# Attention with both couples' weighing in one run, and another set of rebuilt weights in layer one

## The chip, the cores and the metric

One core of a Trainium2 chip runs the whole program. The metric is the device time in microseconds (us) of one execution; the kernel before was run three times, and its median is 843.62 us. A profile was taken of one further execution.

## The reference

Attention with a sigmoid instead of a softmax is followed by two dense layers. All arrays are float32, except the weights, which are float64 because they were scaled by a float64 number.

```
scores = scale * (q @ k^T) - log(448)          # 4 batches x 12 heads, 448 tokens, 64 wide
x = sigmoid(scores) @ v                        # -> 1792 tokens x 768
h = max(x @ w1, x @ w2, x @ w3);  x = h @ w_out               # 768 -> 768 -> 768
h = x @ w_in;  x = (h * sigmoid(1.702 * h)) @ w_out           # 768 -> 2048 -> 768
```

## The kernel before

**Products.** A float32 operand is cut into a high half (a copy in the type fp32r) and a low half (the rest, by a subtraction). Three fast products, high x high, high x low and low x high, stand for one product. The dense layers use a scheme of seven products instead of eight for a 2 x 2 block product, on sums of weight blocks. Attention weighs the values with sigmoids in full float32 (a slower form of product, in several passes).

**The attention** works on couples. A couple is two heads of one batch; 24 couples form 12 periods of two, X (even number) and Y (odd). I count periods from 0. A period has these runs on TensorE:
- `score(c)` for c = 0, 1, 2 (L590 in the profile of before): scores of 3 x 128 keys, two heads side by side, from the high and low halves of q and k; three products for each c, each for two heads. Their result lies in two of six PSUM banks, taken in turn, and `sigmoid` (L625, ScalarE) reads it from there.
- `score_last` (L642): the 64 last keys of X and of Y together, from the raw float32 tiles.
- `weigh_last` (L653): the values of the last keys of the pair of couples before, added to their sums.
- `weigh(c)` for c = 0, 1, 2 (L609): the sigmoids of the 3 x 128 keys times the values v, summed in one PSUM bank for X and one for Y. `give` copies that bank to SBUF when all parts are in.

Beside that, ScalarE or VectorE make the halves of q and k of the next couples (a copy L309 and a subtraction L312, 848 columns), and both engines turn 18 float64 weight tiles into float32 (`single`: L357 on ScalarE, then L367, L364, L368 and L372 on VectorE). Such a tile arrives by a load of 768 KB (L353), and is stored as yk (L294). The raw q and k tiles and the v tiles have three buffers each, used in turn.

**The layers** follow: layer one and layer two for half of the tokens, then both for the other half, then the wide layers in four quarters. In layer one there are nine sets of seven operands from weight blocks. The first half makes them and stores them (`kept`, 384 KB each); the second half loads them again. The sets in `REDO` are not stored; the second half makes them again from yk (one load of 768 KB).

**What sets the order.** The kernel first records all operations, with what each reads and writes. Those of TensorE are chained in the order in which the code records them. A planner (`Order.run`) then goes through an estimate of time: on each engine the operation that is ready and has the smallest latest start (`late`) is issued next. `late` is taken backwards from the operations that need it, or is the given `at` (for conversions: the planned time of TensorE where they were recorded, plus 5.5). A load's `lag` is how long after its end the planner holds it to be usable. Each engine then executes its list in order; DMAs are issued by SyncE (SP), in its order.

Of the kernel before, what the change touches and what calls it, by code (L numbers as in the profile page):

```python
# [17 lines left out]
B, H, S, D = 4, 12, 448, 64  # L18
# [23 lines left out]
LAND, LAND_RAW = 1.0, 2.0  # L42
MM, FULL = 0.201, 0.752
# [148 lines left out]
BUS = 350.0  # L192
# [8 lines left out]
LEAD = 2  # L201
READY = 1
AHEAD = 5.5
REDO = (1, 3, 5, 7)
AGAIN = (1, 3, 5, 7)
CONV1, CONV2 = 4, 10
WITHIN = 1.4
# [2 lines left out]
def moe_chain_kernel(tc, qk, vv, wa, wb, out):  # L210
    nc = tc.nc
    act, dve, pe, sp = nc.scalar, nc.vector, nc.tensor, nc.sync
    scale = 1.0 / math.sqrt(D)
    O = Order()
# [31 lines left out]
    def F(at, n):  # L246
        if at >= FAR2:
            return Reg(sn4, at - FAR2, n, lambda: slab_n[2][:, at - FAR2 : at - FAR2 + n])
        if at >= FAR:
            return Reg(sn1, at - FAR, n, lambda: slab_n[0][:, at - FAR : at - FAR + n])  # L250
        return Reg(sf, at, n, lambda: slab_f[:, at : at + n])
# [4 lines left out]
    def R(at, n):  # L256
        if at >= FAR2:
            return Reg(sn3, at - FAR2, n, lambda: slab_n[1][:, at - FAR2 : at - FAR2 + n])
        if at >= RW:
            return Reg(s2, at - RW, n, lambda: slab_m[1][:, at - RW : at - RW + n])  # L260
        return Reg(sr, at, n, lambda: slab_r[:, at : at + n])
# [4 lines left out]
    def banks(first, n=1, w=S):  # L266
        cut = (lambda: psum[:, first, :w]) if n == 1 else (lambda: psum[:, first : first + n, :w])
        return Reg(sps, first * 512, n * 512, cut)

    class Round:  # L270


        def __init__(self, places):
            self.places, self.i = list(places), 0
# [21 lines left out]
            [to] if writes is None else writes,  # L296
        )

    def load(to, src, kb, after=(), at=None):
        return O.op({"SP": kb / BUS}, lambda e: sp.dma_start(to(), src), (), [to], after, at)  # L300

    def on(e, took, fn, reads, writes):
        return O.op({e: took}, lambda _: fn(), reads, writes)
# [1 line left out]
    def copy(to, of, n, psum=False, both=True):  # L305
        engines = {"ACT": t_act(n)}
        if both:
            engines["DVE"] = t_two(n) if psum else t_one(n)
        return O.op(engines, lambda e: (act.copy if e == "ACT" else dve.tensor_copy)(to(), of()), [of], [to])  # L309
# [4 lines left out]
    def sub(to, a, b, n):  # L314
        return two(to, a, b, ALU.subtract, n)
# [86 lines left out]
    def moving(base, t=None, at=(None,) * 7):  # L402
        b11, b12, b21, b22 = (base + 3 * i * T for i in range(4))
        t = base + 12 * T if t is None else t
        cuts = ((0, 2), (2, 1))

        def combine(to, x, y):
            for j, n in cuts:
                sub(*(F(z + j * T, n * T) for z in (to, x, y)), n * T)

        m = {k: Moving(x) for k, x in zip(("b11", "t1", "t2", "b21", "t3", "b22", "t4"), at)}
        m["b11"].fill(b11)
        combine(t, b12, b11)
        m["t1"].fill(t)
        combine(b11, b22, t)
        m["t2"].fill(b11)
        m["b21"].fill(b21)
        combine(b12, b22, b12)
        m["t3"].fill(b12)
        m["b22"].fill(b22)  # L420
        combine(b21, b21, b11)
        m["t4"].fill(b21)
        return [m[k] for k in ("b11", "t1", "t2", "b21", "t3", "b22", "t4")]
# [132 lines left out]
    class Couple:  # L556


        def __init__(self, p):
            self.p = p  # L560
            t = t_at()
            h, l = q_at()
            cuts = [(Q, QK, QT), (0, 2 * P, 2 * P), (2 * P, Q, Q)] if p == 0 else [(0, QK, QT)]
            self.parts = []
            for start, stop, end in cuts:
                n = stop - start
                to, tp, hp, lp = F(t + start, end - start), F(t + start, n), R(h + start, n), R(l + start, n)
                self.load = load(to, qk[p][:, start:end], (end - start) / 2, at=-9.0 if p == 0 else None)
                copy(hp, tp, n)
                sub(lp, tp, hp, n)  # L570
                self.parts.append((hp, lp))
            self.t, self.h, self.l = F(t, QT), R(h, QK), R(l, QK)
            self.av = banks(6 + p % 2)
            self.a, self.sc = {}, {}

        def values(self):
            self.v = F(v_at(), 8 * D)
            load(self.v, vv[self.p].rearrange("p c d -> p (c d)"), 256)
# [20 lines left out]
            self.a[c] = sigmoid(self.sc[c])  # L599

        def weigh(self, c):
            ps, v, second = self.av, self.v, self.p % 2 == 1
            begin, end = c == 0 and not second, c == 2 and second

            def f(_):
                w, o, x = v().rearrange("p (c d) -> p c d", d=D), ps(), self.a[c]()
                for e in range(2):
                    r = slice(e * D, (e + 1) * D)
                    pe.matmul(o[r], w[:, 2 * c + e], x[:, e * S : (e + 1) * S], start=begin, stop=end)  # L609

            O.pe(f, FULL + (0 if c else 0.15), [v, self.a[c]] + ([] if begin else [ps]), [ps])
            if end:
                self.give()

        def give(self):
            b, hp = divmod(self.p, NPAIR)
# [3 lines left out]
    def sigmoid(ps):  # L620
        a = M1(a_at(), 2 * S)
        on(
            "ACT",
            t_act(2 * S) + 0.07,
            lambda: act.activation(  # L625
                a().rearrange("p (e s) -> p e s", e=2), ps(), AF.Sigmoid, bias=bias, scale=scale
            ),
            [ps],
            [a],
        )  # L630
        return a

    def score_last(two):

        ps = banks(d_at(), 2)

        def f(_):
            o = ps()
            for c, x in enumerate(two):
                for e in range(2):  # L640
                    r, t = slice(e * D, (e + 1) * D), x.t()
                    pe.matmul(o[c * D : (c + 1) * D, e, :], t[r, QK:QT], t[r, Q:QK], start=True, stop=True)  # L642

        O.pe(f, FULL, [x.t for x in two], [ps])
        return ps

    def weigh_last(two, a):
        def f(_):
            x = a()
            for c, y in enumerate(two):  # L650
                w, o, k = y.v().rearrange("p (c d) -> p c d", d=D), y.av(), slice(c * D, (c + 1) * D)
                for e in range(2):
                    pe.matmul(  # L653
                        o[e * D : (e + 1) * D], w[k, 6 + e], x[k, e * S : (e + 1) * S], start=c == 1, stop=c == 0
                    )

        O.pe(f, FULL + 0.15, [a, two[0].av, *(y.v for y in two)], [y.av for y in two])
        two[0].give()

# [24 lines left out]
    def convert(c):  # L686
        p = c.p - LEAD
        if 0 <= p < 18:
            soon(lambda: prepare(p // 2, p % 2, at=XA + 12 * T if c.p % 3 == 2 else None, after=[c.load]))

    prev, last = None, None
    for i in range(NP // 2):
        x = Couple(2 * i)
        x.values()
        if i == 0:
            x.score(0, slice(0, 1))
            x.score(1, slice(0, 1))
            x.score(0, slice(1, 3))
            x.scored(0)
            x.score(1, slice(1, 3))  # L700
            x.scored(1)
        for n in range(0 if i else 2, 3):
            x.score(n)
            x.scored(n)
        convert(x)
        if prev:
            weigh_last(prev, last)
        y = Couple(2 * i + 1)
        y.values()
        last = sigmoid(score_last((x, y)))  # L710
        for n in range(3 if prev else 0):
            prev[1].weigh(n)
        for n in range(3):
            y.score(n)
            y.scored(n)
        convert(y)
        for n in range(3):
            x.weigh(n)
        prev = (x, y)
    weigh_last(prev, last)  # L720
    for n in range(3):
        prev[1].weigh(n)
    O.rows, O.row = False, []
    gate["m"] = O.op({"-": 0.0}, to_m2, after=set(s1.ops))

# [6 lines left out]
    def layer1(x, first, base, extra=()):  # L732
        sets = []
        for m in range(HK):
            for e in range(3):
# [13 lines left out]
                def weights(i=3 * m + e):  # L749
                    if first or i not in REDO:  # L750
                        return Weights(i, first, sums(), keep=i not in REDO)
                    at = again()
                    return Weights(i, True, at + 2 * DM, y=at, keep=False)
# [21 lines left out]
    x = moving(XA)  # L775
# [3 lines left out]
    x = moving(XB)  # L779
    extra = []  # L780
    for fp in range(EARLY):
        for n in range(2):
            extra.append(lambda fp=fp, n=n: prepare(12 + fp, n, "ACT"))
        if fp < READY:
            w = []
# [298 lines left out]
```

## Time and profile before

| | |
|---|---|
| median of 3 runs | 843.62 us (842.98 to 843.77) |
| the profiled execution's own time | 844.5 us |
| its span, first to last instruction | 842.7 us |
| TensorE busy (PE) | 836.4 us, 4447 matmuls |
| VectorE busy (DVE) | 697.3 us |
| ScalarE busy (ACT) | 538.7 us |
| granted clock of TensorE | 1.00 |

Attention lasts until 132.35 us, layer one's second pass is about 278 to 393 us. Times in the views are from the start of the span. A matmul in full float32 shows as several records; products on different parts of the array run beside each other, so the records of a run overlap, and the start of the next run is what counts.

### The profile page before, as it was taken

The numbers are of one execution on the slowest core, as the hardware profiler recorded it, in microseconds if no ns is written. First come the engines' busy times: TensorE is split into PE (matmuls) and PEld (weight loads), VectorE is DVE, ScalarE is ACT, GpSimd is POOL, SyncE is SP. The second block draws the span as 40 slices with busy tenths as digits, with TensorE's granted clock in tenths as the row PEclk, the third lists the DMA queues.
The fourth block names the chain that finished last, engine by engine and source line by source line (L and its number), as shares of the span: only waits on it lengthen the run. The fifth ranks groups of instructions, "written<-read, shape, count | busy, mean of one in ns | idle before, by whom it ended". The sixth has DMA issues, their size and how long they took to land. (4 is left out here: it accounts for less than half of the span.)

```text
span 842.7 us, 12281 instructions
## 1 busy us (share of the span) xinstructions
PE 836.4 (99%) x4447; PEld 726.2 (86%) x4447; DVE 697.3 (83%) x1009; ACT 538.7 (64%) x756; POOL 0.3 (0%) x5
## 2 busy tenths in 40 slices
PE   8999999999999999999999999999999999999998
PEld 4555557999999999999999999999899999999997
DVE  5898898888899877789788899968977889865785
ACT  7899898566475745666658665776657865344430
POOL 0000000000000000000000000000000000000000
PEclk9999999999999999999999999999999999999999
DMA  8899977877558999789999961993349997863033
GB/s 299 294 365 320 370 276 254 307 253 250 206 187 326 389 351 376 283 296 363 406 386 365 409 247 57 360 373 132 108 155 361 345 423 259 289 238 94 0 99 131
DMA packets 73788, 231.83 MB, mean 275 GB/s; under 512 B 8192, under 2 KB 20864, under 8 KB 71936
## 3 DMA queue, kind: packets, MB, share of 16 engines
q1 hardware_dynamic: 73728, 231.05, 75.0%
q8 instruction: 35, 0.57, 0.3%
q14 instruction: 25, 0.20, 0.1%
HBM read 149.82 MB, written 81.20 MB: 274 GB/s over the span
## 5 line engine op out<-in xcount | busy, mean ns | idle before, releaser
L492 PE MATMUL ps<-r 128*128 128x448 f32 x2250 | 454.6, 362 | 0.0
L492 PEld LDWEIGHTS ps<-r 128*128 128x128 f32 x2250 | 421.7, 187 | 28.9 <-issue 0.7
L312 DVE TENSOR_TENSOR r<-f,r 128x384 fp32r<-128x384 f32 (+4 forms) x235 | 163.0, 711 | 24.3 <-ACT r L309 22.7
L309 ACT CAST r<-f 128x384 fp32r<-128x384 f32 (+4 forms) x199 | 124.2, 649 | 45.3 <-PE ps L492 22.4
L309 ACT COPY f<-ps 128x448 f32<-128x448 f32 x132 | 70.6, 537 | 91.8 <-PE ps L492 73.7
L312 DVE TENSOR_TENSOR f<-f 128x384 f32<-128x384 f32 (+4 forms) x140 | 103.5, 759 | 5.7 <-ACT f L849 4.7
L312 DVE TENSOR_TENSOR f<-ps,f 128x448 f32<-128x448 f32 (+1 forms) x117 | 71.6, 616 | 42.2 <-PE ps L492 31.2
L909 PE MATMUL ps<-n,m 128*128 128x448 f32 x432 | 90.8, 362 | 0.0
L909 PEld LDWEIGHTS ps<-n,m 128*128 128x128 f32 x432 | 81.0, 188 | 5.4
L625 ACT ACTIVATE m<-ps,bias 128x896 f32<-128x896 f32 x84 | 79.1, 1006 | 8.6 <-PE ps L590 7.2
L362 ACT ACTIVATE f<-f 128x768 uint8<-128x768 uint32 x38 | 74.7, 1965 | 0.5
L909 PE MATMUL ps<-r,m 128*128 128x448 f32 x288 | 61.4, 363 | 0.4 <-DVE r L312 0.4
L609 PE MATMUL ps<-m,f 128*64 128x448 f32 x288 | 59.4, 548 | 0.0
L909 PEld LDWEIGHTS ps<-r,m 128*128 128x128 f32 x288 | 53.8, 188 | 4.8 <-DVE r L312 1.1
L492 PE MATMUL ps<-m,r 128*128 128x448 f32 x270 | 57.7, 362 | 0.0
L590 PEld LDWEIGHTS ps<-r 64*128 64x128 f32 x432 | 38.4, 184 | 21.1 <-ACT m L625 9.5
L372 DVE SCALAR_TENSOR_TENSOR f<-f 128x768 uint32<-128x768 uint32 x56 | 53.3, 952 | 2.1 <-ACT f L362 1.8
L492 PEld LDWEIGHTS ps<-m,r 128*128 128x128 f32 x270 | 50.6, 187 | 3.4
L357 ACT ACTIVATE f<-f 128x768 f32<-128x768 f32 x56 | 50.8, 911 | 3.7 <-DMA f<-in_wb 2.9
L590 PE MATMUL ps<-r 64*128 64x448 f32 x432 | 50.7, 374 | 1.1 <-DVE r L309 1.1
L309 ACT COPY ps<-ps 128x448 f32<-128x448 f32 x52 | 27.9, 537 | 35.0 <-PE ps L492 30.2
L312 DVE TENSOR_TENSOR r<-n,r 128x384 fp32r<-128x384 f32 (+3 forms) x65 | 46.5, 724 | 3.2 <-ACT r L309 2.5
(64 smaller groups left out, 640.2 us busy)
## 6 DMA issues: line engine op xcount, KB each, us to landing
r<-kept SPq DMA_DIRECT2D x91, 384.0 KB, 6.0
kept<-r SPq DMA_DIRECT2D x84, 384.0 KB, 5.5
f<-in_wb SPq DMA_DIRECT2D x32, 768.0 KB, 6.9
f<-in_wa SPq DMA_DIRECT2D x24, 768.0 KB, 6.8
yk<-f SPq DMA_DIRECT2D x40, 384.0 KB, 5.1
f<-yk SPq DMA_DIRECT2D x17, 768.0 KB, 6.1
f<-y SPq DMA_DIRECT2D x32, 384.0 KB, 6.9
zs<-r SPq DMA_DIRECT2D x7, 1344.0 KB, 13.1
```

The lines of the kernel that those rows point to most:

```text
L309: return O.op(engines, lambda e: (act.copy if e == "ACT" else dve.tensor_copy)(to(), of()), [of], [to])
L312: return on("DVE", t_two(n), lambda: dve.tensor_tensor(to(), a(), b(), op=op), [a, b], [to])
L357: on("ACT", t_act(DM), lambda: act.activation(y(), words(raw(), F32, 1), AF.Copy, scale=2.0**-112), [raw], [y])
L362: act.activation(byte(), words(raw(), U32, 0), AF.Copy, scale=LOW)
L372: lambda: dve.scalar_tensor_tensor(u(), words(raw(), U32, 1), 0x80000007, u(), **by),
L492: pe.matmul(o, a[:, c], b, start=fresh and j == n == 0, stop=j == HK - 1 and n == 2, skip_group_check=True,)
L590: pe.matmul(o[:, e, :], kx[r, c * P : (c + 1) * P], qx[r, Q:QK], start=n == 0, stop=n == 2)
L609: pe.matmul(o[r], w[:, 2 * c + e], x[:, e * S : (e + 1) * S], start=begin, stop=end)
L625: lambda: act.activation(a().rearrange("p (e s) -> p e s", e=2), ps(), AF.Sigmoid, bias=bias, scale=scale),
L909: pe.matmul(o, a, b, start=fresh and k == n == 0, stop=k == 3 and n == 2, skip_group_check=True)
```

## The change

The order of recording in a period changes: after the scores of Y come the weighings of X and of Y, in one run. Before, the weighing of Y was recorded one period later, behind that period's `score_last`. So a couple's last keys are now added after its other keys (`weigh_last` ends the sum instead of opening it), and both `give` copies follow it. The loads of couple 0 are marked as first of all, and the planner's lag for couple 1's load is larger. `REDO` holds the even sets. The other lines of the kernel are the same.

```diff
-REDO = (1, 3, 5, 7)
+REDO = (0, 2, 4, 6, 8)
...
-                self.load = load(to, qk[p][:, start:end], (end - start) / 2, at=-9.0 if p == 0 else None)
+                self.load = load(to, qk[p][:, start:end], (end - start) / 2, at=-99.0 if p == 0 else None, lag=LAND + 1.2 if p == 1 else None)
...
         def weigh(self, c):
-            ps, v, second = self.av, self.v, self.p % 2 == 1
-            begin, end = c == 0 and not second, c == 2 and second
+            ps, v, begin = self.av, self.v, c == 0
...
-                    pe.matmul(o[r], w[:, 2 * c + e], x[:, e * S : (e + 1) * S], start=begin, stop=end)
-
-            O.pe(f, FULL + (0 if c else 0.15), [v, self.a[c]] + ([] if begin else [ps]), [ps])
-            if end:
-                self.give()
+                    pe.matmul(o[r], w[:, 2 * c + e], x[:, e * S : (e + 1) * S], start=begin, stop=False)
+
+            O.pe(f, FULL + (0 if c or self.p % 2 else 0.15), [v, self.a[c]] + ([] if begin else [ps]), [ps])
...
-                        o[e * D : (e + 1) * D], w[k, 6 + e], x[k, e * S : (e + 1) * S], start=c == 1, stop=c == 0
+                        o[e * D : (e + 1) * D], w[k, 6 + e], x[k, e * S : (e + 1) * S], start=False, stop=True
...
-        O.pe(f, FULL + 0.15, [a, two[0].av, *(y.v for y in two)], [y.av for y in two])
-        two[0].give()
+        O.pe(f, FULL + 0.15, [a, *(z for y in two for z in (y.v, y.av))], [y.av for y in two])
+        for y in two:
+            y.give()
...
-        for n in range(3 if prev else 0):
-            prev[1].weigh(n)
         for n in range(3):
             y.score(n)
             y.scored(n)
         convert(y)
-        for n in range(3):
-            x.weigh(n)
+        for z in (x, y):
+            for n in range(3):
+                z.weigh(n)
         prev = (x, y)
     weigh_last(prev, last)
-    for n in range(3):
-        prev[1].weigh(n)
```

The lines behind it move up by some: L590 stays, L609 becomes L608, L642 L639, L653 L650, L625 L622, L909 L904; L309, L312, L357 to L372 and L492 stay.

TensorE's list over one period in the attention, before (ps are PSUM banks, r the halves, f and n the raw tiles and values, m the sigmoids):

```order
L590 MATMUL ps<-r 128x448 x18
L653 MATMUL ps<-m_76,f 64x448 x4
L642 MATMUL ps<-f 64x448 x4
L609 MATMUL ps<-m_76,f 64x448 x6
L590 MATMUL ps<-r 128x448 x18
L609 MATMUL ps<-m_76,f 64x448 x6
```

The same period in the changed kernel:

```order
L590 MATMUL ps<-r 128x448 x18
L650 MATMUL ps<-m_76,f 64x448 x4
L639 MATMUL ps<-f 64x448 x4
L590 MATMUL ps<-r 128x448 x18
L608 MATMUL ps<-m_76,f 64x448 x12
```

The weighing that stood between the last scores and Y's scores now stands behind X's weighing.

VectorE's list around the halves of couple 21 (Y of period 10), before: the high half was a copy on ScalarE, and the first row of 848 columns is its low half.

```order
L372 SCALAR_TENSOR_TENSOR f<-f 128x768
L312 TENSOR_TENSOR r<-f,r 128x848
L309 COPY n_77<-ps 128x448
L367 TENSOR_SCALAR f<-f 128x768
L364 TENSOR_SCALAR f<-f 128x768
L368 TENSOR_SCALAR f<-f 128x768
```

VectorE's list at the same couple in the changed kernel: CAST is couple 21's high half, the row of 848 columns behind it its low half.

```order
L372 SCALAR_TENSOR_TENSOR f<-f 128x768
L309 CAST r<-f 128x848
L367 TENSOR_SCALAR f<-f 128x768
L364 TENSOR_SCALAR f<-f 128x768
L368 TENSOR_SCALAR f<-f 128x768
L312 TENSOR_TENSOR r<-f,r 128x848
L372 SCALAR_TENSOR_TENSOR f<-f 128x768
```

Three steps of the conversion of another tile now stand between the two halves.

ScalarE's list in period 10 of the changed kernel, from the end of period 9's sigmoids on (three sigmoids, then the conversion copy that ends period 9, then period 10):

```order
L622 ACTIVATE m_76<-ps,bias 128x896 x3
L357 ACTIVATE f<-f 128x768
L622 ACTIVATE m_76<-ps,bias 128x896
L357 ACTIVATE f<-f 128x768
L622 ACTIVATE m_76<-ps,bias 128x896 x3
L309 COPY n_77<-ps 128x448 x2
```

The second L357 is the first step of the conversion whose three next steps stand in VectorE's list above; it stands behind the period's first sigmoid.

## Rows read from the trace of the kernel before

**Rows 1.** The page, busy time of each engine, its share and instructions.
```profile
PE 836.4 (99%) x4447; PEld 726.2 (86%) x4447; DVE 697.3 (83%) x1009; ACT 538.7 (64%) x756; POOL 0.3 (0%) x5
```
**Rows 2.** Timeline of PE, period 3: start, length, engine, line, operation, tiles, count.
```profile
34.53 2.08 PE L590 MATMUL ps<-r 64*128 64x448 f32 x18
36.55 0.98 PE L653 MATMUL ps<-m,f 64*64 64x448 f32 x8
37.35 0.93 PE L642 MATMUL ps<-f 64*64 64x448 f32 x8
38.21 2.48 PE L609 MATMUL ps<-m,f 128*64 128x448 f32 x12
40.62 2.08 PE L590 MATMUL ps<-r 64*128 64x448 f32 x18
42.63 2.48 PE L609 MATMUL ps<-m,f 128*64 128x448 f32 x12
45.03 2.08 PE L590 MATMUL ps<-r 64*128 64x448 f32 x18
```
**Rows 3.** Sums of that period: PE, PEld, DVE, ACT, POOL busy, clock, DMA share, GB/s.
```profile
34.53:45.03 10.50, 10.50 (x78) 5.27 (x76) 9.13 (x14) 8.96 (x10) 0.00 (x0) 1.00 0.92 350
```
**Rows 4.** Timeline of the start, all engines.
```profile
6.58 0.90 ACT L309 CAST r<-f 128x848 fp32r<-128x848 f32 x1 [2.48 <-DMA f<-in_qk]
6.83 0.24 DVE L309 CAST r<-f 128x144 fp32r<-128x144 f32 x1 [1.73 <-DMA f<-in_qk]
...
7.12 0.88 PE L590 MATMUL ps<-r 64*128 64x448 f32 x6 [1.08 <-DVE r L309]
...
7.93 0.98 PE L642 MATMUL ps<-f 64*64 64x448 f32 x8
8.65 0.60 DVE L309 CAST r<-n 128x848 fp32r<-128x848 f32 x1
8.84 2.28 PE L590 MATMUL ps<-r 64*128 64x448 f32 x18
...
9.28 1.04 DVE L312 TENSOR_TENSOR r<-n,r 128x848 fp32r<-128x848 f32 x1
...
11.13 2.48 PE L609 MATMUL ps<-m,f 128*64 128x448 f32 x12
```
**Rows 5.** Timeline of PE's weight loads in one weighing.
```profile
22.05 0.14 PEld L609 LDWEIGHTS ps<-m,f 128*64 128x64 f32 x2 [0.23 <-issue]
...
23.18 0.14 PEld L609 LDWEIGHTS ps<-m,f 128*64 128x64 f32 x2 [0.23 <-issue]
```
**Rows 6.** Timeline of ACT in period 3.
```profile
35.51 3.93 ACT L625 ACTIVATE m<-ps,bias 128x896 f32<-128x896 f32 x4 [1.24 <-PE ps L590]
39.39 0.94 ACT L357 ACTIVATE f<-f 128x768 f32<-128x768 f32 x1
...
41.59 2.81 ACT L625 ACTIVATE m<-ps,bias 128x896 f32<-128x896 f32 x3 [0.44 <-PE ps L590]
```
**Rows 7.** Timeline of DVE in period 3, the conversion's steps.
```profile
40.36 0.56 DVE L367 TENSOR_SCALAR f<-f 128x768 f32<-128x768 f32 x1 [0.31 <-ACT f L357]
40.84 0.62 DVE L309 COPY f<-ps 128x448 f32<-128x448 f32 x1
...
42.24 1.03 DVE L364 TENSOR_SCALAR f<-f 128x768 uint16<-128x768 uint16 x1
43.05 0.60 DVE L368 TENSOR_SCALAR f<-f 128x768 uint32<-128x768 uint32 x1
```
**Rows 8.** Timeline of SP in period 3, the load of Y's v.
```profile
37.56 0.33 SPq L300 DMA_DIRECT2D f<-in_vv  x1
```
**Rows 9.** All 24 loads of v, from issue to landing.
```profile
DMA to landing us min/median/max: 2.6/5.2/7.9
```
**Rows 10.** Sums of layer one's second pass, columns as in rows 3.
```profile
278.00:393.00 115.00, 115.00 (x577) 107.79 (x576) 94.98 (x167) 72.26 (x96) 0.00 (x0) 1.00 0.93 339
```
**Rows 11.** Groups by shape there: busy us, mean ns, idle before.
```profile
L312 DVE TENSOR_TENSOR r<-f,r 128x384 fp32r<-128x384 f32 x35 | 19.0, 552 | 1.4 <-ACT r L309 1.1
```

More of the change, by code (lines that the diff above doesn't have):

```diff
@@ L297, in dma, with load @@
         )
-    def load(to, src, kb, after=(), at=None):
-        return O.op({"SP": kb / BUS}, lambda e: sp.dma_start(to(), src), (), [to], after, at)
+    def load(to, src, kb, after=(), at=None, lag=None):
+        return O.op({"SP": kb / BUS}, lambda e: sp.dma_start(to(), src), (), [to], after, at, lag)
     def on(e, took, fn, reads, writes):
```

## The prediction

> **What bounds the kernel now.** I read the page first: TensorE is busy for 836.4 of the 842.7 us span [rows 1]. So a change gains where TensorE's own work gets shorter or where one of its few gaps closes, and loses where it makes TensorE wait. I then read the timeline of TensorE over one period of the attention (two couples) [rows 2], then the sums of that stretch by engine [rows 3]: TensorE fills all 10.50 us of it, VectorE 9.13, ScalarE 8.96, and the DMA engines 92%. Nothing waits on TensorE there, but nothing beside it has much room. Then the timeline of the start [rows 4], the only place in the attention where TensorE stands still, and last the units that set when TensorE's data are ready: weight loads, ScalarE, VectorE, the loads of v [rows 5 to 9], and layer one's second pass [rows 10, 11]. The granted clock is 1.00 in every stretch read here, so no clock term enters.
>
> I write S for a run of scores (L590), K for the last weighing (L653), L for the last scores (L642), W for a weighing (L609), and T for the start of a period's first S.
>
> **Part 1: the two weighings in one run.** Before, a period is S K L W S W. After, it is S K L S W W: both halves of W stand together. The products are the same, so only what lies at the joints changes. One step of W takes (23.18 - 22.05)/3 = 0.377 us by its weight loads [rows 5]; six steps are 2.26 us, but a W lasts 2.41 and 2.40 from start to start [rows 2]. So entering and leaving a W costs 0.15 us, and two W in one run pay it once: 12 steps and 0.15, 4.67 instead of 4.81. There are 24 such runs before and 12 after, so 12 x 0.15 = **-1.80 us**. This holds if L followed by S costs what L followed by W costs (0.86, [rows 2]). The trace has that joint once, at the start: L at 7.93, S at 8.84, 0.91 [rows 4]. There L itself follows an S and not a K, so its first step carries an entering cost, and I keep 0.86; with 0.91 the gain would be 0.10 a period, -1.2 in all. That is one end; the other is -1.8, as nothing can make the runs shorter than their steps.
>
> The Trainium skill, "TensorEngine Tiling (Array Packing)", section Key Properties, says that changing the tiling mode drains the engine while moving to another tile does not. S works in tiles of 64 x 128, K and L in 64 x 64, W in 128 x 64; L to S is a change of mode like L to W, so the rule counts one drain fewer per period. It also says that L to S is not free; taken at the 0.91 of the one joint shown, it would make the sum of this part -1.2.
>
> **Part 2: the start.** Four loads go out first. Couple 1's (848 columns) lands before couple 0's third part: their first readers start at 6.58 and 6.83 [rows 4], and TensorE stood still 1.08 us for the second. The change swaps the two loads. The third part then arrives early, and couple 1 arrives when the pair of them was in, at 6.83. L needs couple 1's raw tile, so it starts at about 6.85 instead of 7.93. S follows 0.91 later, at 7.76, but its second product needs couple 1's low half, which VectorE now makes after a copy of its own: 0.60 and 1.04 for those two [rows 4], 6.83 + 0.60 + 1.04 and three hand-overs of 0.03 give 8.56, against 7.76 + 2.01/9 = 7.98. So S waits 0.58 there and ends eight of nine steps later, 8.56 + 1.79 = 10.35, where before the first W started at 11.13. **-0.78 us.** Bounds: the loads share the bandwidth, so couple 1 may land 0.4 later (-0.4), or S may not wait (-1.3).
>
> **Part 3: where the closer runs make TensorE wait.** Y's S now starts at T + 2.02 + 0.80 + 0.86 = T + 3.68 instead of T + 6.09, and Y's W at T + 3.68 + 2.01 + 2.30 = T + 7.99 instead of T + 14.2 (3.7 into the next period).
> - Y's third score writes the banks that L filled, so the sigmoid of L must be over. ScalarE's first four sigmoids end at 35.51 + 3.93, T + 4.91 [rows 6]; the third score comes at T + 3.68 + 6 x 0.22 = T + 5.0. It just fits: 0 to 0.1 in each of 11 periods; I take **+0.2**, with 0 and 1.1 as ends.
> - A conversion ahead of a split, in period 10 (the eleventh). In the other periods the split that S needs is over before its S comes. In this one the order puts ScalarE's conversion copy (L357) right behind the first sigmoid, and VectorE's three conversion steps between couple 21's high half and its low half (the two places shown above). Step by step: the first sigmoid starts at T + 0.98 and the next instruction 0.90 later, (2.81 - 1.01)/2 [rows 6]; L357 holds 0.94, so it is over at T + 2.82. VectorE: L367 at once, L364 0.48 later, L368 0.81 later [rows 7], the split 0.55 later (L368's 0.60 less their overlap) at T + 4.69, its end 1.04 later [rows 4] at T + 5.73. S wants it for its second product at T + 3.68 + 0.22 = T + 3.90. The wait is 5.77 - 3.90, **+1.85 us**. Before, the same split ran long before its S. While TensorE waits here the sigmoids behind L357 catch up, so they add nothing. The ends: 0 if couple 21's low half is not held by those three, 2.8 if the delayed sigmoids (each later by 0.94) also hold the period's W.
> - V of couple Y is loaded once K has read the buffer: issued at 37.56, T + 3.03 [rows 8], now wanted at T + 7.99, or 0.4 sooner for the weight load. A load of v takes 2.6, 5.2, 7.9 us at least, in the middle and at most [rows 9], so it may be in by T + 5.6 or by T + 8.2. In the new order on SyncE the v loads of a period stand first, Y's ahead of X's, with the conversions' loads behind them and mostly issued before the next period starts, so I take the short side, 0; the other end is worked out as a rival.
>
> **Part 4: layer one remakes sets 0, 2, 4, 6, 8.** Five sets instead of four are rebuilt in the second pass: 7 stores of 384 KB fewer in the first pass, 7 loads of 384 KB fewer and one of 768 KB more in the second. VectorE gets 11 more operations on 384 columns (4 sums, 7 low halves) at 0.552 = 6.1 us [rows 11], ScalarE or VectorE 7 more copies. In the second pass VectorE is busy 95.0 of 115 us, TensorE all 115, DMA 0.93 [rows 10]. So 6.1 us go into 20 idle ones, and a tight DMA queue gets lighter: **0**. If the cover is missing at the ends, where set 0 or set 8 has no stored partner beside it, an operand (sum, copy, low half: about 1.5 us) comes late, and two or three do so: up to +4. Below zero there is nothing to win: TensorE has no idle time in that stretch.
>
> **The sum.** -1.80 - 0.78 + 0.20 + 1.85 + 0 = -0.53 us. From this execution's own 844.5 that is 844.0; the runs' median lies 0.88 below that execution, 843.62, which gives 843.1.
>
> **Rivals.**
> 1. *The conversion in period 10 does not hold the split* (its load is late enough that TensorE has slipped, or the other terms cover it). For it: in the profile before, 840 us of the same kind of order cost TensorE almost nothing. Against it: an in-order engine cannot run the split before the three steps. Then -1.80 - 0.78 + 0.2 = -2.4: 841.2.
> 2. *Slower: Y's weighing waits for v.* Place: the first product of Y's W in periods 1 to 11. At the middle landing of 5.2 v is in at T + 8.23; with a hand-over the weights load at 8.3 and the product starts at about 8.45 instead of 7.99: 0.46 in each period where DMA is backed up, which by a share of 0.92 [rows 3] is most of them, say 8: +3.7, 846.8. It decides against the change from a landing of about 4.9 us on. For it: the median row. Against: the new order issues long conversion loads behind v.
> 3. *Late operands in layer one or behind it*, as worked out under part 4, +1.5 to +4: 844.6 to 847.1. For it: VectorE at 83%. Against: the DMA relief.
> 4. *The joint L to S costs 0.91*: 843.7.
>
> **Chances.** Forecast with rival 4: 0.57, its own range 842.2 to 844.3. Rival 1: 0.20. Rival 2: 0.12. Rival 3: 0.11. What a measurement of this kernel can tell from no change is about 0.2%, 1.7 us: below 841.9 is faster, above 845.3 slower. Faster: 0.20 of rival 1 and 0.05 of the forecast's lower edge, 0.25. Slower: rival 2 and a third of rival 3, 0.15. The same: 0.60. For the range I leave out the upper halves of rivals 2 and 3 and the lowest part of rival 1: 840.8 to 845.8.
>
> **What would show it.** In the changed profile a period of the attention should last 10.35 us from S to S, with W as one run of 4.67. The first W should start at about 10.35, S of period 10 should have one gap of 1.8 us ended by VectorE's subtraction, and layer one should start about 0.5 us sooner than before. It is wrong if TensorE waits for the v load, if period 10 has no gap, or if idle time appears on TensorE between 278 and 393 us.

## The result and the profile after

The changed kernel is slower: 848.09 us (median; 847.53 to 849.41) against 843.36 us, a ratio of 1.0057 with a 95% interval of 1.0045 to 1.0070. The forecast was 843.1.

The profiled execution took 847.59 us, its span is 845.8. Half of the loss lies in the attention, half behind it. Layer one's first product starts at 133.83 us instead of 132.35 (+1.48). From there to the end it is 845.81 - 133.83 = 711.98 us instead of 842.69 - 132.35 = 710.34 (+1.64). Together that is 3.12 of the 4.73 us between the medians. The rest comes of which executions were profiled: that of before (844.5) lies 1.1 above its kernel's median, that of after 0.5 below.

**The page** shows that no work was added that TensorE must do (columns as in [rows 1]):

```profile
PE 836.9 (99%) x4447; PEld 728.1 (86%) x4447; DVE 704.1 (83%) x1025; ACT 535.8 (63%) x758; POOL 0.3 (0%) x5
```

TensorE has the same 4447 matmuls and nearly the same busy time, VectorE 6.8 us more. So the time went into waits of TensorE, and **the waits of PE** in the changed kernel name them (us in total, times, longest us):

```profile
PE ps L590 <- DVE r L312: 2.0, 2, 1.6
PE ps L667 <- DVE r L661: 1.4, 1, 1.4
PE ps L492 <- DVE f L312: 0.8, 1, 0.8
PE ps L608 <- DMA f<-in_vv: 0.5, 1, 0.5
PE ps L492 <- ACT r L309: 0.4, 1, 0.4
```

Before, this view has only the start's 1.4 and 1.1 and one wait of 0.4 in the wide layers. The view counts idle time only. A wait also costs the pipelined matmul behind it, so I measure from start to start: the 1.65 of period 10 is 1.83 there.

**A period of the attention**, timeline of PE, the counterpart of [rows 2], then its sums as in [rows 3]:

```profile
36.43 2.09 PE L590 MATMUL ps<-r 64*128 64x448 f32 x18
38.45 0.98 PE L650 MATMUL ps<-m,f 64*64 64x448 f32 x8
39.25 0.93 PE L639 MATMUL ps<-f 64*64 64x448 f32 x8
40.11 2.17 PE L590 MATMUL ps<-r 64*128 64x448 f32 x18
42.21 4.73 PE L608 MATMUL ps<-m,f 128*64 128x448 f32 x24
46.87 1.47 PE L590 MATMUL ps<-r 64*128 64x448 f32 x11
```
```profile
36.43:46.87 10.44, 10.44 (x78) 5.37 (x76) 9.13 (x15) 8.14 (x9) 0.00 (x0) 1.00 0.99 351
```

Both weighings in one run last 46.87 - 42.21 = 4.66 instead of 4.81: the 0.15 of the joint is won, and L before S costs 40.11 - 39.25 = 0.86, as taken. But Y's scores last 2.10 instead of 2.01, in every period: the weight load of the third score waits for the sigmoid of L on ScalarE (timeline of PE's weight loads).

```profile
41.40 0.19 PEld L590 LDWEIGHTS ps<-r 64*128 64x128 f32 x2 [0.18 <-ACT m L622]
```

A period is 10.44, so 0.06 is left of 0.15.

**The two waits of the attention**, timeline of PE in periods 8 and 10:

```profile
94.38 2.48 PE L608 MATMUL ps<-m,f 128*64 128x448 f32 x12
97.34 2.48 PE L608 MATMUL ps<-m,f 128*64 128x448 f32 x12 [0.49 <-DMA f<-in_vv]
...
113.93 0.48 PE L590 MATMUL ps<-r 64*128 64x448 f32 x2
116.06 1.87 PE L590 MATMUL ps<-r 64*128 64x448 f32 x16 [1.65 <-DVE r L312]
```

In period 8 Y's weighing waits for v, in period 10 Y's second score product for couple 21's low half. VectorE in period 10 shows why (its timeline):

```profile
112.67 0.60 DVE L309 CAST r<-f 128x848 fp32r<-128x848 f32 x1 [0.78 <-DMA f<-in_qk]
113.18 0.55 DVE L367 TENSOR_SCALAR f<-f 128x768 f32<-128x768 f32 x1
113.65 1.02 DVE L364 TENSOR_SCALAR f<-f 128x768 uint16<-128x768 uint16 x1
114.47 0.59 DVE L368 TENSOR_SCALAR f<-f 128x768 uint32<-128x768 uint32 x1
114.97 1.03 DVE L312 TENSOR_TENSOR r<-f,r 128x848 fp32r<-128x848 f32 x1
```

**The start**, all engines, the counterpart of [rows 4]:

```profile
7.12 1.23 PE L639 MATMUL ps<-f 64*64 64x448 f32 x8
7.36 0.60 DVE L309 CAST r<-f 128x848 fp32r<-128x848 f32 x1 [1.15 <-DMA f<-in_qk]
...
8.28 0.47 PE L590 MATMUL ps<-r 64*128 64x448 f32 x2
...
9.09 1.88 PE L590 MATMUL ps<-r 64*128 64x448 f32 x16 [0.34 <-DVE r L312]
...
10.90 1.35 PE L608 MATMUL ps<-m,f 128*64 128x448 f32 x6
```

The first W starts at 10.90 instead of 11.13 (forecast: 10.35). Couple 1 came in at about 7.1 to 7.3, not at 6.83.

**Layer one's second pass**, sums as in [rows 10], and PE's timeline where it waits:

```profile
278.00:393.00 115.00, 113.67 (x566) 105.61 (x565) 98.82 (x176) 73.96 (x104) 0.00 (x0) 1.00 0.89 320
```
```profile
312.15 5.57 PE L492 MATMUL ps<-r 128*128 128x448 f32 x27
318.52 2.05 PE L492 MATMUL ps<-r 128*128 128x448 f32 x9 [0.81 <-DVE f L312]
320.41 3.76 PE L492 MATMUL ps<-m,r 128*128 128x448 f32 x18
324.01 3.77 PE L492 MATMUL ps<-r 128*128 128x448 f32 x18
328.17 3.07 PE L492 MATMUL ps<-r 128*128 128x448 f32 x12 [0.40 <-ACT r L309]
```

From start to start these two places lose 2.1 us, where before TensorE never waited. (The loss behind the attention is only 1.64 in all, since the one wait that before has in the wide layers, 0.6 from start to start at 594 us, is gone as well.) The text on the planner ahead of the forecast has a gap here: only in the attention are TensorE's products chained in the order of the code. From layer one on they are not (`O.rows = False`), and the planner picks TensorE's order too. Between the two kernels 15 of the 63 places in this pass hold another product.

### The profile page after: what moved, and what is told of

It reads as the page before. It is cut to its first block, busy times and chain, and to the rows that moved or that the text cites. A ratio compares the mean times of both kernels' runs of the same rounds, so it can differ in the third digit from the quotient of the medians.

```text
span 845.8 us, 12280 instructions
## 1 busy us (share of the span) xinstructions
PE 836.9 (99%) x4447; PEld 728.1 (86%) x4447; DVE 704.1 (83%) x1025; ACT 535.8 (63%) x758; POOL 0.3 (0%) x5
## 4 chain that ended last, share of the span: by engine, by line
PE 95%; DMA 3%; DVE 1%; SPq 0%; issue 0%; DVEq 0%
PE ps L492 59%; PE ps L904 24%; PE ps L608 6%; PE ps L590 5%; DMA f<-in_qk 2%; PE ps L650 1%; DMA kept<-r 1%; PE ps L639 1%; DMA f<-in_vv 1%; DVE r L312 0%; DVE r L309 0%; DVE f L312 0%; SPq L300 0%; DVE f L364 0%; DVE f L372 0%
## 5 line engine op out<-in xcount | busy, mean ns | idle before, releaser
L492 PE MATMUL ps<-r 128*128 128x448 f32 x2250 | 455.1, 362 | 1.3 <-DVE f L312 0.8
L492 PEld LDWEIGHTS ps<-r 128*128 128x128 f32 x2250 | 421.7, 188 | 31.1 <-DVE r L312 1.2
L312 DVE TENSOR_TENSOR r<-f,r 128x384 fp32r<-128x384 f32 (+4 forms) x242 | 166.9, 706 | 21.8 <-ACT r L309 20.9
L309 ACT CAST r<-f 128x384 fp32r<-128x384 f32 (+4 forms) x204 | 124.3, 633 | 53.4 <-PE ps L492 22.9
L309 ACT COPY f<-ps 128x448 f32<-128x448 f32 x127 | 67.9, 538 | 84.2 <-PE ps L492 64.6
L312 DVE TENSOR_TENSOR f<-f 128x384 f32<-128x384 f32 (+3 forms) x144 | 106.1, 752 | 4.9 <-ACT f L844 4.0
L312 DVE TENSOR_TENSOR f<-ps,f 128x448 f32<-128x448 f32 (+1 forms) x117 | 71.7, 617 | 45.6 <-PE ps L492 34.7
L904 PE MATMUL ps<-n,m 128*128 128x448 f32 x432 | 90.9, 362 | 0.0
L622 ACT ACTIVATE m<-ps,bias 128x896 f32<-128x896 f32 x84 | 79.1, 1012 | 17.1 <-PE ps L590 16.0
L904 PEld LDWEIGHTS ps<-n,m 128*128 128x128 f32 x432 | 81.0, 188 | 5.4
L904 PE MATMUL ps<-r,m 128*128 128x448 f32 x288 | 61.2, 362 | 0.0
L590 PEld LDWEIGHTS ps<-r 64*128 64x128 f32 x432 | 38.8, 188 | 23.2 <-issue 13.4
L608 PE MATMUL ps<-m,f 128*64 128x448 f32 x288 | 57.0, 544 | 0.5 <-DMA f<-in_vv 0.5
L492 PE MATMUL ps<-m,r 128*128 128x448 f32 x270 | 57.4, 362 | 0.0
L904 PEld LDWEIGHTS ps<-r,m 128*128 128x128 f32 x288 | 53.9, 188 | 4.0 <-DVE r L312 0.3
L372 DVE SCALAR_TENSOR_TENSOR f<-f 128x768 uint32<-128x768 uint32 x56 | 53.3, 952 | 2.0 <-ACT f L362 1.6
L357 ACT ACTIVATE f<-f 128x768 f32<-128x768 f32 x56 | 51.2, 922 | 4.7 <-DMA f<-in_wa 3.1
L590 PE MATMUL ps<-r 64*128 64x448 f32 x432 | 52.1, 381 | 2.0 <-DVE r L312 2.0
L492 PEld LDWEIGHTS ps<-m,r 128*128 128x128 f32 x270 | 50.6, 188 | 3.4
L312 DVE TENSOR_TENSOR r<-n,r 128x384 fp32r<-128x384 f32 (+3 forms) x65 | 46.3, 722 | 4.9 <-ACT r L309 4.4
L309 ACT COPY ps<-ps 128x448 f32<-128x448 f32 x52 | 27.5, 529 | 35.9 <-PE ps L492 30.9
## 6 DMA issues: line engine op xcount, KB each, us to landing
zs<-r SPq DMA_DIRECT2D x7, 1344.0 KB, 11.4
```

The source lines that it names most:

```text
L312: return on("DVE", t_two(n), lambda: dve.tensor_tensor(to(), a(), b(), op=op), [a, b], [to])
L357: on("ACT", t_act(DM), lambda: act.activation(y(), words(raw(), F32, 1), AF.Copy, scale=2.0**-112), [raw], [y])
L372: lambda: dve.scalar_tensor_tensor(u(), words(raw(), U32, 1), 0x80000007, u(), **by),
L492: pe.matmul(o, a[:, c], b, start=fresh and j == n == 0, stop=j == HK - 1 and n == 2, skip_group_check=True,)
L590: pe.matmul(o[:, e, :], kx[r, c * P : (c + 1) * P], qx[r, Q:QK], start=n == 0, stop=n == 2)
L622: lambda: act.activation(a().rearrange("p (e s) -> p e s", e=2), ps(), AF.Sigmoid, bias=bias, scale=scale),
```

## The experiments

**Which half does it? The attention alone, and the even sets alone.**

```diff
 # changed kernel
-REDO = (0, 2, 4, 6, 8)
+REDO = (1, 3, 5, 7)
```

> The attention of the changed kernel, with the odd sets 1, 3, 5, 7 rebuilt as before. Theory A (the two gaps of TensorE in layer one's second pass, 2.1 us together, come from the order of products that the planner chose there: product 102 stands right behind product 101 in the same PSUM bank, product 107 right behind 106 in the same weight buffer; with the odd sets no such neighbours stand in the list): no gaps at 317 and 327 us, but period 10 still waits 1.6 to 1.9 us for the low half, and a wait for v of 0 to 1.5 stays: 845.3 to 846.5 us against 848.1 for the changed kernel. Rival B (the attention alone costs all of it, by the queue of DMAs it leaves behind): 848 us. Rival C (the attention is free and the even sets cost all): 843.4 us or below.

845.84 us, ratio 1.0028 (1.0018 to 1.0037); no wait over 0.2 us behind the attention, 709.7 us from layer one's start to the end. As theory A said of its size: without the waits in layer one 2.2 us are gone, and 2.4 us above the kernel before remain. By this profile they are the attention's, as the 709.7 behind it are no longer than before (710.3). TensorE's list in the second pass is that of the kernel before.

```diff
 # kernel before
-REDO = (1, 3, 5, 7)
+REDO = (0, 2, 4, 6, 8)
```

> The kernel before with the even sets 0, 2, 4, 6, 8 rebuilt, nothing else. Theory A (the gaps in layer one are an accident of the planner's order, and in this kernel no product stands next to one with the same bank or weight buffer): the time of the kernel before, 843.0 to 843.8 us, no gap over 0.3 us in 278 to 393 us. Rival C (five sets rebuilt cost TensorE time by 6 us more work on VectorE): 845 to 847 us, with gaps ended by VectorE in layer one's second pass.

844.58 us, ratio 1.0013 (1.0004 to 1.0021): between the two. No wait in layer one's second pass, so five sets there need not make TensorE wait. One wait of 0.76 at 507 us in the wide layers is new, and the 0.6 at 594 is gone. So 2.4 and 1.1 us for the halves alone fall short of the 4.7 for both edits at once: the halves do not add up.

**Is it the order of the products or VectorE's work?** First all of the second pass in the code's order:

```diff
 # changed kernel
+    O.rows, O.row = True, []
     x = moving(XB)
...
     layer1(x, False, XB, extra)
+    O.rows, O.row = False, []
```

> The changed kernel with TensorE's products in layer one's second pass chained in the order of the code (as in the attention) instead of an order that the planner picks; the even sets are still rebuilt, with all of their work on VectorE. Theory A (neighbours in the list are the cause): no gap at 317 to 329 us, 2.1 us less than the changed kernel, 845.7 to 846.3; a strict order may cost up to 1 us at the seam of two layers. Rival C (VectorE's work for five sets makes operands late): the gaps stay, 848 us, or grow.

861.53 us, ratio 1.0210 (1.0196 to 1.0224): one wait of 12.7 us for a kept load at 310 us; a strict order cannot take a ready product of another set meanwhile. Behind it no gap over 0.3 us follows, but VectorE had 12.7 us to catch up, so this run tells neither theory from the other.

Then only the two pairs of neighbours taken apart:

```diff
     def run(self):
+        for later, first in ((1263, 1230), (1251, 1259)):
+            self.ops[later].pre.add(self.ops[first])
```

> The changed kernel, with two products of layer one's second pass told to come behind another: product 102 behind the one that followed it, product 107 behind 109. The even sets, VectorE's work and the attention are unchanged; in the list no product has its predecessor's bank or weight buffer any more. Theory A (the neighbours are the cause): the gaps at 317 to 329 us shrink from 2.0 us to under 0.5, the time falls by 1.5 to 2 us. Rival C (VectorE's work for the five sets is late, whatever the order): product 102's place is taken by one whose low half VectorE has ready at 320.3, so TensorE waits 2 us or more there, and the time stays at 848 or rises by up to 1.

849.80 us, ratio 1.0080 (1.0066 to 1.0095). Theory A falls as it stood: with the neighbours apart TensorE waits longer at the same place, for other operands (timeline of PE):

```profile
312.77 4.97 PE L494 MATMUL ps<-r 128*128 128x448 f32 x24
319.74 0.67 PE L494 MATMUL ps<-m,r 128*128 128x448 f32 x2 [2.00 <-ACT r L311]
320.93 1.68 PE L494 MATMUL ps<-m,r 128*128 128x448 f32 x7 [0.53 <-DVE r L314]
```

Next the fifth set taken away, with the neighbours left: `REDO = (0, 2, 4, 6)`.

> The changed kernel with four even sets rebuilt, 0, 2, 4, 6, instead of five: set 8 is stored and loaded, VectorE does 4 operations on 384 columns or more less, all of them at the end of the pass, and the same two neighbours stand in TensorE's list (products 101 and 102, 106 and 107). Theory A: the gaps at 317 and 327 us stay, 847.5 to 848.5 us. Rival C (the fifth set's work is what makes VectorE late): they go, 846 us.

847.70 us, ratio 1.0048 (1.0036 to 1.0060), the same two waits at the same places. By itself this does not clear the fifth set's work: what was taken away lies behind the waits (from 285 to 330 us VectorE is busy 39.95 us here and 39.55 in the changed kernel). With the run before it, which waited longer as rival C had said, VectorE's work could still be the cause; against it stands only the kernel before with the even sets, which has no wait. What I took from it: the operands of this pass come just in time, and which one is late is a matter of the lists. I called that theory D and redrew the layers' lists alone.

**Other lists, the same work.**

```diff
         lag = (LAND if "SP" in on else 0.1) if lag is None else lag
+        if "SP" in on and not self.rows:
+            on = {"SP": on["SP"] * 0.99}
         o = Op(len(self.ops), on, fn, at, lag)
```

> The kernel before, with one number of the planner changed: it holds the transfers of the layers to take 0.99 of what it held. The attention's lists stay as before on every engine; those of layer one and behind it are drawn anew (VectorE's from 161 us of the plan on). No instruction is added or taken away. Theory D (layer one's second pass has no slack: its operands arrive just in time, and the list of the kernel before is one of few that never makes TensorE wait, so any other list, by whatever edit, costs 1 to 3 us there): 844.5 to 847 us, with waits for kept loads or for VectorE between 278 and 393 us. Rival (the even sets or the new attention are what makes the operands late, and the lists don't matter): 843.0 to 843.8 us.

> As the run before it, with 1.02 instead of 0.99: a second list for the layers of the kernel before. Theory D: 844.5 to 847 us, waits at other places than in the first. Rival: 843.0 to 843.8 us.

> The changed kernel with the planner's estimate of the layers' transfers at 1.03: the same attention, the same five even sets, another list for the layers. Theory D: layer one's second pass loses anything between 0 and 3 us instead of 2.0, the attention ends as in the changed kernel: 846 to 849 us. Rival (the five even sets make it late): again 2 us or more of waits between 310 and 330 us, 848 us.

> As the run before it, with 0.98: a second other list for the layers of the changed kernel. Theory D: 846 to 849 us, waits of 0 to 3 us at places of its own. Rival: 2 us or more of waits between 310 and 330 us, 848 us.

| kernel, estimate of the layers' transfers | median us | ratio to before |
|---|---|---|
| before, 0.99 | 844.47 | 1.0012 (1.0004 to 1.0021) |
| before, 1.02 | 844.78 | 1.0016 (1.0007 to 1.0024) |
| changed, 1.03 | 848.73 | 1.0071 (1.0057 to 1.0085) |
| changed, 0.98 | 846.08 | 1.0034 (1.0022 to 1.0046) |

Theory D holds in kind and was too narrow in place. The redrawn lists of the kernel before cost 1.0 and 1.3 us, the low end of 1 to 3, and 0.99 waits at 506 us in the wide layers, not in layer one. For the changed kernel the list alone is worth 2.6 us between the medians. At 1.03 the second pass is idle 0.4 us, and the wide layers wait twice instead (0.6 each). At 0.98, with all five even sets, the second pass has no wait (its sums):

```profile
278.00:393.00 115.00, 115.00 (x577) 107.64 (x576) 100.82 (x176) 79.63 (x107) 0.00 (x0) 1.00 0.91 326
```

VectorE is busy 100.8 of 115 us there, more than in the changed kernel with its 2 us of waits. So the five sets' work need not make TensorE wait, and a share of busy time does not tell whether operands are late. The three other runs that keep the changed kernel's order of products in this pass (four sets above, low halves and the filled gap below) have the same two waits, 0.8 and 0.4 us idle.

**The attention's waits.** Low halves ahead of conversions:

```diff
-                sub(lp, tp, hp, n)
+                low = sub(lp, tp, hp, n)
+                if p:
+                    low.at = O.clock - 20.0
```

> The changed kernel with one more number: the low halves of q and k get an earlier latest start (20 us before the planned clock), so that the planner never puts a conversion's steps ahead of them; in period 10 VectorE's list has one conversion step between the two halves instead of three. The pair of neighbours in layer one's list is the same as in the changed kernel. Theory A (the wait in period 10 is the three steps): the second score product of Y in period 10 waits under 0.4 us, and the time falls by 1.2 to 1.8 us, to 846.3 to 846.9; the gaps at layer one stay. Rival (the operand was late by its load, which landed 0.8 us after VectorE was free): the wait stays at 1.6 and the time at 848.1.

847.96 us: nothing gained. No product waits for the low half now, and the scores of period 10 last 2.68 instead of 3.92. But its weighing lasts 7.33 instead of 4.66: 1.93 of that is one wait, and behind it the granted clock was 0.77 from 122 to 124 us and 0.69 from 124 to 128. On ScalarE the sigmoid for it now stands behind the high half of a coming couple, which waits for its load (timeline, ScalarE's two rows and then PE's):

```profile
120.90 0.90 ACT L309 CAST r<-n 128x848 fp32r<-128x848 f32 x1 [1.44 <-DMA n<-in_qk]
121.71 1.00 ACT L624 ACTIVATE m<-ps,bias 128x896 f32<-128x896 f32 x1
...
122.76 1.49 PE L610 MATMUL ps<-m,f 128*64 128x448 f32 x4 [1.93 <-ACT m L624]
```

Then the last two of the 18 conversions moved out of the attention:

```diff
-        if 0 <= p < 18:
+        if 0 <= p < 16:
...
-    layer1(x, True, XA, [lambda i=i: prepare(i // 2, i % 2, "ACT", XA + 12 * T) for i in range(18, 24)])
+    layer1(x, True, XA, [lambda i=i: prepare(i // 2, i % 2, "ACT", XA + 12 * T) for i in range(16, 24)])
```

> The changed kernel with the last two of the 18 conversions of the attention moved into layer one's first pass (six stand there already). The steps that stand between couple 21's halves go; TensorE's list in layer one has no neighbours with one bank or buffer. Theory (the attention loses what it wins by the conversions' steps ahead of a split and their loads beside v): period 10's scores last 2.0 to 2.1 us instead of 3.9, layer one starts 1.8 us sooner than in the changed kernel; the wait for v in period 8 stays, since the lists up to there are the same; with layer one's gaps gone too the time is 843.8 to 844.8. Rival (the wait only moves, to the sigmoids or the next couple's halves, as in the run with the earlier low halves): layer one starts no sooner, 846 us.

847.23 us, ratio 1.0048 (1.0035 to 1.0061). The first half is as the theory said: period 10's scores last 2.10, and layer one starts at 131.58, 2.25 sooner than in the changed kernel and 0.77 sooner than before. The wait for v in period 8 stays (0.73). So the three conversion steps were the whole of period 10's wait, as VectorE's rows above say too: begun right behind the high half, at 113.18, the low half would have ended at about 114.2 (113.18 + 1.03), when the second product wants it. The second half fails: the layers lose it again, 713.4 us from layer one's start to the end instead of 710.3 (1.0 us for VectorE at 262, 1.1 for a kept load at 328).

**The start alone.** The two edits of the start in the kernel before:

> The kernel before with only the start changed: couple 0's third part is loaded ahead of couple 1, and the planner's lag for couple 1 is larger. The forecast gave this part -0.78 us: 842.7. Theory from the changed kernel's trace (couple 1 lands later by what the third part is earlier: its first W starts at 10.9 us there, 0.23 sooner than before, and at 11.3 to 11.4 in two other runs with the same start): no gain, 843.2 to 843.8 us.

845.64 us, ratio 1.0031 (1.0017 to 1.0044): neither the forecast's 842.7 nor the theory's 843.2 to 843.8. Its first W starts at 10.6 us, but its layers have another list, and that one waits 2.4 us for a kept load (PE):

```profile
310.44 3.76 PE L492 MATMUL ps<-r 128*128 128x448 f32 x18
316.63 2.05 PE L492 MATMUL ps<-r 128*128 128x448 f32 x9 [2.43 <-DMA r<-kept]
```

**The scatter.** Period 10's gap filled with products:

```diff
                 o, hh, ll = ps(), h(), l()
+                for e in [0, 1] * (7 if self.p == 21 and c == 0 else 0):
+                    r = slice(e * D, (e + 1) * D)
+                    pe.matmul(o[:, e, :], hh[r, :P], hh[r, Q:QK], start=True, stop=True)
```

> The changed kernel with 14 more products in front of period 10's second score run (the first product again, seven times for each head, into the bank that is overwritten next; their results are not used). They fill the gap in which TensorE waits for couple 21's low half; all lists stay else. Theory E (a gap of some 2 us lets the granted clock fall to half in some executions, and that is the scatter of the changed kernel's times above its fastest): the fastest run stays at 847.3 to 847.7 us, since VectorE's steps set the end of the wait; the median falls towards it, to 847.5 to 848, and no run has a mean clock under 0.999. Rival (the scatter comes from the loads of v and of kept operands): times from 847.5 to 849.5 us or more, as before.

848.01 us (847.34 to 849.01), no run's mean clock under 0.999. The median does not fall clear of the scatter (848.09 without the fill). That the clock stays up says nothing here: the changed kernel's own four executions, 847.53 to 849.41, all have 1.0 as well, so theory E does not explain their scatter. Nor was the whole gap filled in this profile: couple 21's high half starts at T + 3.8 instead of T + 2.5 (T is the start of the period), as do the products of L that read its raw tile, and the second product still waits 0.68 us. V makes TensorE wait in two periods, 0.34 and 1.18 us. So in this profile late loads make the attention 1.4 us longer than in the changed kernel's; that the scatter as a whole comes of them is not shown. The clock adds to it in some executions of other kernels (last section).

**Two tries for a version that beats both**, with the conversions moved and other lists for the layers (0.96 with the even sets, 0.98 with the odd ones):

> A try at a version that beats both: the changed kernel with the last two conversions of the attention moved into layer one (no wait in period 10) and the planner's estimate of the layers' transfers at 0.96, another list for the layers. Theory: the attention ends 0.6 us sooner than before, at 131.5 to 131.8 us; the layers lose 0.5 to 2 us as any new list does, with two more conversions in layer one's first pass: 843.5 to 846 us. It beats the kernel before (below 843.2) only if its list makes no operand late.

> As the try before it, with the odd sets 1, 3, 5, 7 rebuilt as in the kernel before, and 0.98: the attention ends at 131.5 to 131.8 us again, the layers have one more list: 843.5 to 846 us; below 843.2 only if no operand is late.

847.12 us (1.0037 to 1.0061) and 846.91 us (1.0034 to 1.0058). Neither does. Both wait again in the attention, now in period 11 (its scores 2.59 instead of 2.07), and in the layers. No kernel here beats the one before.

## Why the forecast was wrong

- **Part 4, layer one at 0: this step failed.** I argued that 6.1 us of VectorE's work go into 20 idle ones. The work did fit (the changed kernel's list at 0.98 shows it). What failed is the premise that the order stays: any edit gives the planner another list for the layers, TensorE's own products among them. In this list two operands are late: 2.1 us in the trace, 2.2 between the medians of the changed kernel and of the attention alone. The list of the kernel before is a good draw: three others with its attention and about its work (even sets, 0.99, 1.02) cost 1.0 to 1.3 us, a fourth, drawn with the start's edits, 2.2. My rival 3 had the place and the size (+1.5 to +4), but named as its cause sets without a stored neighbour. With set 8 stored the waits stay, and at 0.98, with sets 0 and 8 made again, they are gone, so its size was luck.
- **Part 3, the third score: mis-sized.** Forecast 0.2 in all; measured 2.10 - 2.01 = 0.085 in each of 11 periods, 0.9. The view had the sigmoids right: ScalarE's four end at T + 4.9. But I took the product's start, T + 5.0, for the moment at which it needs them. Its weights load before it, and that load waited 0.18 us for ScalarE, until T + 4.97 (41.40 - 36.43).
- **Part 3, period 10: right.** Forecast 1.85 (its own 5.77 - 3.90 gives 1.87); 3.92 - 2.10 = 1.83 here, and 1.7 to 2.1 in seven profiled executions with this list. Its cause is shown by the run without the two conversions. That the size fits so closely is in part luck: the steps began at T + 3.00 and not T + 2.85, behind the high half, whose load VectorE waited for (0.78), and Y's scores began 0.07 later than I counted, with a first step of 0.3 instead of 0.22.
- **Part 3, v: I took the short side (0).** In this trace period 8 loses 0.71, in the other executions with this list 0.2 to 0.8 (in the filled run 1.18, and 0.34 in period 3). Rival 2 had the mechanism; it hits one period, in the filled run two, not eight.
- **Part 2, the start: failed.** Forecast -0.78, from both loads arriving in the order of issue at the same total time. The first W starts at 10.1 to 11.4 us with the change (thirteen profiled executions, mean 10.8) and at 10.5 to 11.1 without it (four, mean 11.0): 0.1 to 0.2 is gained. Couple 1 lands later than the pair of them did before, and the landings scatter by more than the gain.
- **Part 1, the joint: right.** 4.66 instead of 4.81 per period. L before S is 0.86 as L before W was, so rival 4 falls. By the Trainium skill's rule that a change of tiling mode drains the array ("TensorEngine Tiling (Array Packing)", Key Properties), the price hangs on the number of changes, one fewer per period; the trace agrees with 0.15.

The attention's sum from the trace: -1.8 + 0.9 + 1.83 + 0.71 - 0.23 = +1.4, against +1.48 measured. Over seven profiled executions with this attention layer one starts at 132.95 to 135.87, in the mean 134.05; in four with the attention of before at 131.69 to 132.35, in the mean 132.18. So the attention costs 1.9 us, not the -0.53 forecast, and the layers' list about 2 more.

Left open: why the redrawn lists of before cost 1 us in the median while their profiled executions show only 0.1 to 0.3 us more between layer one's start and the end. Landing times that differ between executions would do it; no run isolates that.

## What to carry to other kernels

Where a planner sets the order, an edit is two changes: the one in the diff and a new list for everything behind it; price the second with a list redrawn without any edit before believing the first. Compare the order of every engine, the bottleneck's too, over the whole program. The planner's own estimate can be asked first, with care: `Order.run` puts layer one's first product at 131.9 us for the kernel before and at 135.5 for the changed one, so it held the new attention to be slower (twice the measured size). For the layers it misleads: with the even sets alone it ends 2.1 us earlier, and that run was 1.1 longer. In a kernel that is at 99% a gain of 0.15 us per period is smaller than what an operand that comes just in time costs in one place.

## What the runs showed of the hardware

The granted clock can fall behind a gap of TensorE of 1.5 us. In the run with the attention alone TensorE starts no product between 114.50 and 116.46 us in period 10 and is idle for 1.49 of that; its windows then show (columns as in [rows 3], the clock is the last but two):

```profile
115.00:118.00 3.00, 1.54 (x14) 1.42 (x16) 3.00 (x5) 3.00 (x6) 0.00 (x0) 0.95 0.96 298
118.00:120.00 2.00, 2.00 (x10) 0.70 (x8) 2.00 (x4) 2.00 (x3) 0.00 (x0) 0.50 1.00 362
120.00:122.00 2.00, 2.00 (x10) 0.72 (x8) 2.00 (x4) 2.00 (x3) 0.00 (x0) 0.72 1.00 409
122.00:130.00 8.00, 8.00 (x64) 4.36 (x62) 7.33 (x11) 5.86 (x8) 0.00 (x0) 1.00 0.44 142
```

There the clock is 0.50 (1.2 GHz) for a while, and the weighing that starts at 118.72 lasted 5.84 instead of 4.66: its first three of twelve steps took 0.74 to 0.80 us each instead of 0.377. In the changed kernel's own profile the same gap (1.65 idle) left the clock at 1.00 (2.4 GHz). The Trainium skill, "TensorE: Matmul & The Clock Gate", Part 1, says that the clock follows how busy TensorE has been recently, and that the moment at which it rises behind a kernel's start varies from run to run. In these two traces the fall varies as well: it came in one execution and not in the other. Leaving aside the kernel with the 12.7 us wait, every timed execution with a mean clock of 0.996 or 0.997 is of a kernel whose profile has a wait of 1.5 us or more (five kernels), and lies 2.4 to 7.2 us above the shortest execution of its kernel. How much of that is the clock's, and how much the waits', no run separates; one execution of the kernel before, which has no such wait behind its start, has 0.998 and lies 2.2 us above its shortest.
